# Loading the queries of an attention kernel in one transfer over 128 partitions, and moving them to their places with VectorE copies

## The chip, the cores and the metric

The kernel runs on one core of a Trainium2 chip. The metric is the device time of one execution in microseconds (us); a time is the median of several runs. The kernel before took 639.06 us (3 runs, 638.83 to 639.22). A ratio of two kernels is the mean time of one kernel's fast runs over that of the other's fast runs of the same rounds, so it is not quite the ratio of the medians that are quoted.

## The reference

The reference is plain softmax attention with few queries and many keys: 128 heads (8 x 16), 16 queries each, 2048 keys and values each, head size 256, all in bf16.

```python
B, H, Sq, Skv, Dh = 8, 16, 16, 2048, 256
def reference(q, k, v):
    scale = q.shape[-1] ** -0.5
    scores = jnp.einsum('bhqd,bhkd->bhqk', q, k) * scale
    attn = _softmax(scores, axis=-1)
    return jnp.einsum('bhqk,bhkd->bhqd', attn, v)
```

K and V are 134 MB each, the queries 1.05 MB, the output 1.05 MB. Every byte of K and V is used once (the page counts 269.48 MB read from HBM), and the work is mostly moving bytes: DMA is 72% of the chain that ended last.

## The kernel before

The kernel handles 8 heads at a time (a group g of 16), in two halves e = 0, 1 ("units", u = 2g + e) of 4 MB of K and 4 MB of V each. All K and V loads are issued by SyncE, in one order, each waiting only until its place in SBUF is free. A K load may start when VectorE has transposed the K that was in its place (`kt`); a V load when TensorE has used up the V before it.

```python
qx = q.rearrange("b h s d -> (b h s) d").rearrange("(u a s) d -> a u (s d)", a=4, s=SQ)
...
QR = VB[:, 1, 0:SQ, :].rearrange("p s d -> p (s d)")     # the raw queries, in a V buffer not yet used

def emit_qload(eng, a):                                   # head 4u+a goes to partition 32a+u
    return eng.dma_start(QR[32 * a:32 * a + 2 * G, :], qx[a])

def emit_qt(eng):                                         # VectorE: transposes each 32x32 block
    return eng.transpose(QT[:].bitcast(F32), QR.bitcast(F32))
...
j_q = [J(("sp", "sp", "act", "act")[a], "ldq", lambda eng, a=a: emit_qload(eng, a), [j_qz], dma=(sem_q, 64)) for a in range(4)]
...
# K, groups 0 and 1: two halves of 2 MB per unit; later groups: one load of 4 MB
[("kt", g - 1, e, 2 * h + 1)] if g else []                # what a K load waits for
# order on VectorE at the start: qt, then kt(0, e, c) for both units, then the first row maximum
```

The queries thus come in four loads: load `a` takes every fourth head (32 KB apart in HBM, 8 KB each) and writes the 32 partitions from 32a on. Two of them are issued by SyncE ahead of all K loads, two by ScalarE. After the transpose, ScalarE scales the queries into the weights of TensorE (`qwb`), 8 instructions per group.

## Time and profile before

| what | value | where |
|---|---|---|
| time | 639.06 us | runs |
| span of the profiled run | 637.7 us | page, head |
| TensorE, VectorE, ScalarE busy | 76%, 67%, 15% | page, part 1 |
| DMA | 90% or more in all slices but the first and the last | page, part 2 |
| rate, whole span | 424 GB/s | page, part 2 |

From the page of the kernel before, the head and two rows of part 2 (the span in 40 slices of 16 us: busy tenths of the DMA engines, and what they moved):

```profile
span 637.7 us, 5071 instructions
DMA  8999999999999999999999999999999999999996
GB/s 311 429 443 428 426 430 440 430 438 434 432 428 432 432 428 432 430 430 430 431 443 438 432 430 429 430 432 432 428 432 430 440 432 430 432 436 430 417 423 274
```

The stream runs at about 430 GB/s everywhere except in the first and last slice. The DMA part of the same kernel (operation, count, KB each, median us from issue to landing) shows how deep the queue is:

```profile
KN<-in_k_dram SPq DMA_DIRECT2D x28, 4096.0 KB, 30.0
VB<-in_q_dram SPq DMA_DIRECT2D x2, 256.0 KB, 5.0
VB<-in_q_dram ACTq DMA_DIRECT2D x2, 256.0 KB, 6.9
```

A K load of 4 MB lands 30.0 us after its issue, though 4 MB take 9.7 us at 430 GB/s: some 20 us of earlier loads stand ahead of it. By this estimate a compute engine that runs a few us late in the middle does not starve the DMA engines. What can count is a hole in the stream, and the first slice (311 GB/s) has one.

The windows of 1 us from 3 us on, kernel before. Columns: window, its length, then busy us and instruction counts of TensorE, weight loads, VectorE, ScalarE and GpSimd, the TensorE clock, the busy share of the DMA engines, and GB/s:

```profile
3.00:4.00 1.00, 0.00 (x0) 0.00 (x0) 0.00 (x0) 0.00 (x0) 1.00 (x1) 1.00 1.11 295
4.00:5.00 1.00, 0.00 (x0) 0.00 (x0) 0.00 (x0) 0.00 (x0) 0.91 (x1) 1.00 1.07 254
5.00:6.00 1.00, 0.00 (x0) 0.00 (x0) 0.00 (x0) 0.00 (x0) 0.00 (x0) 1.00 1.02 238
6.00:7.00 1.00, 0.00 (x0) 0.00 (x0) 0.00 (x0) 0.00 (x0) 0.00 (x0) 1.00 1.09 270
7.00:8.00 1.00, 0.00 (x0) 0.00 (x0) 0.00 (x0) 0.00 (x0) 0.00 (x0) 1.00 0.93 328
```

The last two columns are the point: the DMA engines count as fully busy, yet move 238 to 328 GB/s, 55 to 76% of the 430 GB/s of later. So here a busy share near 1 does not tell that transfers go at full rate; only the bytes do.

The start in order of time, kernel before (start us, us, engine, line, operation, count, and in brackets the idle time before it and what ended it):

```profile
0.73 0.86 SPq L110 DMA_DIRECT2D VB<-in_q_dram  x2
0.73 0.90 ACTq L110 DMA_DIRECT2D VB<-in_q_dram  x2
1.64 31.96 SPq L212 DMA_DIRECT2D KN<-in_k_dram  x8
9.72 2.31 DVE L113 STREAM_TRANSPOSE QT<-VB 128x2048 f32<-128x2048 f32 x1 [7.65 <-DMA VB<-in_q_dram]
12.07 3.45 ACT L122 ACTIVATE QW<-QT 32x128 bf16<-32x128 bf16 x8 [9.11 <-DVE QT L113]
14.01 4.50 DVE L128 STREAM_TRANSPOSE KB<-KN 128x2048 f32<-128x2048 f32 x2 [1.98 <-DMA KN<-in_k_dram]
18.58 0.61 PE L145 MATMUL S_ps<-KB,QW 128*128 128x512 bf16 x1 [18.58 <-DVE KB L128]
```

The queries arrive only at 9.7 us and the first K half at 14.0. The end of the chain that ended last (start us, us, what):

```profile
593.87 30.26 DMA KN<-in_v_dram
624.27 10.79 PE O_ps L178 x96
```

After the V piece that lands at 624.1 us TensorE works without a break for 10.8 us, and 2.6 us later the program is over. So the start of this last piece of work follows the stream, and the time follows it.

### The profile page before, as it was taken

What the parts mean: (1) busy time and instruction counts of PE and PEld (TensorE: products, weight loads), DVE (VectorE), ACT (ScalarE), POOL (GpSimd) and SP (SyncE); (2) the same over time, 40 slices, a digit from 0 to 9 for tenths busy, and PEclk for the clock granted to TensorE, in tenths of its full rate; (3) what the DMA queues carried; (4) which work ended last, traced back from release to release, by engine and by line L of the source; (5) the groups of instructions that cost most, each with busy time, mean ns of one, the idle gap of its engine ahead of it and who ended that gap; (6) DMA issues with size and microseconds to landing.
All of it is one profiled execution on the core that took longest, in us unless ns stands there. A gap on an engine that the chain in (4) does not pass through costs nothing.

```text
span 637.7 us, 5071 instructions
## 1 busy us (share of the span) xinstructions
PE 485.4 (76%) x2176; PEld 165.5 (26%) x1680; DVE 428.3 (67%) x371; ACT 93.8 (15%) x176; POOL 4.2 (1%) x7
## 2 busy tenths in 40 slices
PE   0747858959599595986959779596895949959897
PEld 0101312314122140321303113131231312314286
DVE  3979494775947669386683957749477594766960
ACT  2030301103020030300303002030120302103010
POOL 2000000000000000000000000000000000000000
PEclk9979998969989798997979979699897998979999
DMA  8999999999999999999999999999999999999996
GB/s 311 429 443 428 426 430 440 430 438 434 432 428 432 432 428 432 430 430 430 431 443 438 432 430 429 430 432 432 428 432 430 440 432 430 432 436 430 417 423 274
DMA packets 13766, 270.62 MB, mean 424 GB/s; under 512 B 1600, under 2 KB 3904, under 8 KB 4416
## 3 DMA queue, kind: packets, MB, share of 16 engines
q1 hardware_dynamic: 13248, 269.83, 98.9%
q10 hardware_dynamic: 512, 0.70, 0.4%
q8 instruction: 4, 0.07, 0.0%
q14 instruction: 2, 0.02, 0.0%
HBM read 269.48 MB, written 1.05 MB: 424 GB/s over the span
## 4 chain that ended last, share of the span: by engine, by line
DMA 72%; DVE 18%; issue 5%; PE 4%; ACT 0%; SPq 0%; DVEq 0%; ACTq 0%
DMA KN<-in_k_dram 67%; DVE KB L128 17%; DMA KN<-in_v_dram 5%; PE O_ps L178 2%; PE S_ps L145 1%; PE S_ps L133 1%; DVE negm L150 0%; ACT QW L122 0%; SPq L110 0%; DVE O_fin L326 0%; SPq L230 0%; DVEq L481 0%; ACT P_sb L154 0%; ACTq L122 0%; ACTq L484 0%
## 5 line engine op out<-in xcount | busy, mean ns | idle before, releaser
L128 DVE STREAM_TRANSPOSE KB<-KN 128x2048 f32<-128x2048 f32 x128 | 284.8, 2281 | 57.1 <-DMA KN<-in_k_dram 56.1
L145 PE MATMUL S_ps<-KB,QW 128*128 128x512 bf16 x528 | 214.3, 414 | 138.3 <-DMA VB<-in_v_dram 95.0
L133 PE MATMUL S_ps<-KB,QW 128*128 128x512 bf16 x496 | 204.8, 413 | 0.0
L172 PE MATMUL O_ps<-VB,PT 128*128 128x512 bf16 x896 | 195.6, 379 | 9.9 <-DMA VB<-in_v_dram 9.9
L145 PEld LDWEIGHTS S_ps<-KB,QW 128*128 128x128 bf16 x528 | 54.0, 103 | 342.4 <-issue 278.8
L172 PEld LDWEIGHTS O_ps<-VB,PT 128*128 128x128 bf16 x896 | 86.7, 98 | 121.6 <-issue 19.0
L150 DVE TENSOR_REDUCE negm<-S_ps 128x1 f32<-128x2048 f32 x16 | 36.7, 2292 | 86.9 <-PE S_ps L133 86.9
L154 ACT ACTIVATE P_sb<-S_ps,negm 128x2048 bf16<-128x2048 f32 x16 | 31.5, 1967 | 410.5 <-DVE negm L150 410.5
L158 DVE STREAM_TRANSPOSE PC<-P_sb 128x1024 bf16<-128x1024 bf16 x32 | 37.9, 1222 | 33.8 <-ACT P_sb L154 33.8
L164 DVE COPY PT<-PC 32x1024 bf16<-32x1024 bf16 x128 | 53.5, 418 | 3.4 <-PE O_ps L178 1.7
L122 ACT ACTIVATE QW<-QT 32x128 bf16 (+1 forms) x128 | 54.0, 422 | 10.4 <-DVE QT L113 9.1
L315 ACT ACTIVATE O_tmp<-O_ps,rab 128x256 f32<-128x256 f32 x15 | 7.1, 473 | 96.9 <-issue 96.9
L178 PE MATMUL O_ps<-KN,PT 128*128 128x256 bf16 x128 | 14.4, 273 | 1.1 <-DMA KN<-in_v_dram 1.1
L178 PE MATMUL O_ps<-VB,PT 128*128 128x256 bf16 x128 | 14.1, 273 | 0.4 <-DVE PT L164 0.4
L178 PEld LDWEIGHTS O_ps<-KN,PT 128*128 128x128 bf16 x128 | 12.4, 98 | 3.0 <-issue 1.3
L178 PEld LDWEIGHTS O_ps<-VB,PT 128*128 128x128 bf16 x128 | 12.4, 98 | 2.3 <-DVE PT L164 0.8
L326 DVE TENSOR_SCALAR O_fin<-O_ps,rab 128x256 bf16<-128x256 f32 x2 | 1.0, 484 | 12.8 <-PE O_ps L178 6.6
L320 DVE SCALAR_TENSOR_TENSOR O_fin<-O_ps,rab,O_tmp 128x256 bf16<-128x256 f32 x15 | 6.7, 448 | 1.8 <-issue 1.8
L113 DVE STREAM_TRANSPOSE QT<-VB 128x2048 f32<-128x2048 f32 x1 | 2.3, 2311 | 7.7 <-DMA VB<-in_q_dram 7.7
L297 DVE TENSOR_SCALAR rab<-mask,rinv 128x2 f32<-128x2 f32 x16 | 3.7, 228 | 1.5
L191 POOL MEMSET PT<- 128x4096 f32 x1 | 3.5, 3511 | 0.0
L301 DVE COPY rab<-rab 128x2 f32<-128x2 f32 x15 | 2.5, 167 | 1.2
(11 smaller groups left out, 8.4 us busy)
## 6 DMA issues: line engine op xcount, KB each, us to landing
VB<-in_v_dram SPq DMA_DIRECT2D x28, 4096.0 KB, 24.3
KN<-in_k_dram SPq DMA_DIRECT2D x28, 4096.0 KB, 30.0
KN<-in_k_dram SPq DMA_DIRECT2D x8, 2048.0 KB, 15.0
VB<-in_v_dram SPq DMA_DIRECT2D x4, 2048.0 KB, 17.4
KN<-in_v_dram SPq DMA_DIRECT2D x2, 2048.0 KB, 28.0
KN<-in_v_dram SPq DMA_DIRECT2D x2, 1024.0 KB, 24.6
KN<-in_v_dram SPq DMA_DIRECT2D x3, 512.0 KB, 27.2
out_dram<-O_fin SPq DMA_DIRECT2D x13, 64.0 KB, 29.8
```

Of the source, the lines that this page charges most:

```text
L122: ins = eng.activation(ap_of(dv, dv.offset + 32 * a + e, [[256, 4], [128, 2], [2, 16]]), src.rearrange("p (s b) t -> p b t s", b=4), ACTF. ...
L128: return eng.transpose(KBf[:, c % R_KB].rearrange("p t i -> p (t i)"), KNf[:, e].rearrange("p t i -> p (t i)")[:, n * c:n * c + n])
L133: return eng.add_instruction(mybir.InstMatmult(start_tensor_calc=start, stop_tensor_calc=stop, ldweights=False, tile_size=(128, 128), tile ...
L145: ins = mm(S_ps[:, 2 * h + c, :], QW[:, e, bp, :], rhs, start=(e == 0 and bp == 0), stop=(e == 1 and bp == 7))
L150: return eng.tensor_reduce(out=negm[:], in_=S_ps[:].rearrange("p c n -> p (c n)"), axis=AX.X, op=ALU.max, negate=True)
L154: return eng.activation(P_sb[:], S_ps[:].rearrange("p c n -> p (c n)"), ACTF.Exp, bias=negm[:], scale=1.0, accum_out=lsum[:])
L158: return eng.transpose(PC[:, h].rearrange("p t x -> p (t x)"), P_sb[:, 1024 * h:1024 * h + 1024])
L164: ins = eng.tensor_copy(PT[pr, 32 * h:32 * h + 32, pr], PC[pr, h])
L172: ins = eng.matmul(O_ps[:, 0, :], PT[:, t, :], rhs, start=(t == 0), stop=(t == NT - 1))
L178: ins = eng.matmul(O_ps[:, bank, 0:D], PT[:, t, :], buf[:, t, :], start=(t == 0), stop=(t == NT - 1))
L315: j_ea[g] = J("act", "ea", lambda eng: eng.activation(O_tmp[:], src, ACTF.Copy, scale=rab[:, 0, 0:1]), [("pv", g, 1) if g < last - 1 else ...
L320: j_eb[g] = J("dve", "eb", lambda eng: eng.scalar_tensor_tensor(out=O_fin[:, 0, :], in0=src, scalar=rab[:, 0, 1:2], in1=O_tmp[:], op0=ALU. ...
```

## The change

Intent: let the queries come in one load, a head to a partition, straight and contiguous, over all 128 partitions. The transpose of 32x32 blocks (one instruction, 2.31 us) then leaves them in the wrong 32 partitions, so VectorE copies them, 32 partitions at a time, to the places where the scaling expects them: four copies per four groups of heads, 16 in all, the first four before the K transposes, the rest in places where VectorE was expected to wait.

```diff
-    qx = q.rearrange("b h s d -> (b h s) d").rearrange("(u a s) d -> a u (s d)", a=4, s=SQ)
+    qx = q.rearrange("b h s d -> (b h) (s d)")
...
-        def emit_qload(eng, a):
-            return eng.dma_start(QR[32 * a:32 * a + 2 * G, :], qx[a])
         def emit_qt(eng):
-            return eng.transpose(QT[:].bitcast(F32), QR.bitcast(F32))
+            return eng.transpose(QN[:].bitcast(F32), QR.bitcast(F32))
+        def emit_qc(eng, x):
+            src = QN[32 * x:32 * x + 32, :].bitcast(F32).rearrange("p (y v a) -> p y v a", v=8, a=4)
+            for a in range(4):
+                dst = QT[32 * a:32 * a + 32, :].bitcast(F32).rearrange("p (y u) -> p y u", u=32)
+                ins = eng.tensor_copy(dst[:, :, 8 * x:8 * x + 8], src[:, :, :, a])
+            return ins
...
-        j_q = [J(("sp", "sp", "act", "act")[a], "ldq", lambda eng, a=a: emit_qload(eng, a), [j_qz], dma=(sem_q, 64)) for a in range(4)]
+        j_q = [J("sp", "ldq", lambda eng: eng.dma_start(QR[0:NH, :], qx), [j_qz], dma=(sem_q, 16))]
...
-                             [("qt", 0), j_qwz, ("qk", g - 1, 1, 1) if g else None])
+                             [("qc", g // 4), j_qwz, ("qk", g - 1, 1, 1) if g else None])
...  # on VectorE: qc(0) after qt; qc(1) before the first row maximum; qc(2), qc(3) at the end of group 1
-                            mine = dict(k) if jb.cls in ("ld", "ldq", "st") else {**prev[e], **k}
+                            mine = dict(k)
+                            if jb.cls not in ("ld", "ldq", "st"):
+                                mine.update((key, val) for key, val in prev[e].items() if k.get(key, 0) < val)
```

The last hunk belongs to the part that plans which waits can be left out; it takes a few waits out of the loops of VectorE and ScalarE. Slots and slices of the loops move along.

More of the change, by code (lines that the diff above doesn't have):

```diff
@@ L14 @@
 R_KB = 4
-PE_SLOT, DVE_SLOT, ACT_SLOT = 8, 144, 80
+PE_SLOT, DVE_SLOT, ACT_SLOT = 8, 160, 80
 STEP = 16
@@ L54, in bass_standalone__softmax_full_bidir__sampling_kernel @@
         QT = ec(nc.sbuf_tensor("QT", [128, SQ * D], BF16))
+        QN = ec(nc.sbuf_tensor("QN", [128, SQ * D], BF16))
         QW = ec(nc.sbuf_tensor("QW", [128, 2, 8, 128], BF16))
@@ L193, in bass_standalone__softmax_full_bidir__sampling_kernel @@
         j_mask = J("dve", "mask", emit_mask, [j_ident])
-        j_qz = J("dve", "qz", lambda eng: eng.memset(QR.bitcast(F32), 0.0)) if 2 * G < 32 else None
-        j_q = [J(("sp", "sp", "act", "act")[a], "ldq", lambda eng, a=a: emit_qload(eng, a), [j_qz], dma=(sem_q, 64)) for a in range(4)]
+        j_qz = J("dve", "qz", lambda eng: eng.memset(QR.bitcast(F32), 0.0)) if NH < 128 else None
+        j_q = [J("sp", "ldq", lambda eng: eng.dma_start(QR[0:NH, :], qx), [j_qz], dma=(sem_q, 16))]
         j_k, j_v, j_kt, j_qk, j_pv = {}, {}, {}, {}, {}
         j_qwb, j_qt, j_exp, j_pt, j_px, j_max, j_rab = {}, {}, {}, {}, {}, {}, {}
-        j_ea, j_eb, j_st, j_rold = {}, {}, {}, {}
+        j_ea, j_eb, j_st, j_rold, j_qc = {}, {}, {}, {}, {}
         vparts = {NU - 4: [32, 32], NU - 3: [32, 32], NU - 2: [32, 32], NU - 1: [16, 16, 8, 8, 8, 4, 2, 2]}
@@ L366, in bass_standalone__softmax_full_bidir__sampling_kernel, with qc @@
         j_qt[0] = J("dve", "qt", emit_qt, j_q)
+        def qc(x):
+            if 32 * x < NH:
+                j_qc[x] = J("dve", "qc", lambda eng: emit_qc(eng, x), [("qt", 0)])
+        qc(0)
         for g in range(G):
@@ L379, in bass_standalone__softmax_full_bidir__sampling_kernel @@
                 px(g - 1, 1)
+            if g == 0:
+                qc(1)
             dve_max(g)
@@ L386, in bass_standalone__softmax_full_bidir__sampling_kernel @@
             small(g)
+            if g == 1:
+                qc(2)
+                qc(3)
         dve_tail = len(order["dve"])
@@ L396, in bass_standalone__softmax_full_bidir__sampling_kernel @@
         tables = {"kt": j_kt, "qwb": j_qwb, "qt": j_qt, "qk": j_qk, "exp": j_exp, "pt": j_pt, "px": j_px, "max": j_max,
-                  "rab": j_rab, "rold": j_rold, "ea": j_ea, "eb": j_eb, "st": j_st, "pv": j_pv}
+                  "rab": j_rab, "rold": j_rold, "qc": j_qc, "ea": j_ea, "eb": j_eb, "st": j_st, "pv": j_pv}
         def resolve(d):
@@ L405, in bass_standalone__softmax_full_bidir__sampling_kernel @@
                  "pe": [order["pe"][0:4]] + [order["pe"][6 * x - 2:6 * x + 4] for x in range(1, last)],
-                 "act": [order["act"][3:5]] + [order["act"][3 * x + 2:3 * x + 5] for x in range(1, last)]}
-        n_tail = {"dve": dve_tail, "pe": 6 * last - 2, "act": 3 * last + 2}
+                 "act": [order["act"][1:3]] + [order["act"][3 * x:3 * x + 3] for x in range(1, last)]}
+        n_tail = {"dve": dve_tail, "pe": 6 * last - 2, "act": 3 * last}
         def plan():
```

## The prediction

> **What bounds the kernel now.** DMA. The page's slices show the DMA engines at 90% or more in all but the first and last of 40, at about 430 GB/s. In the middle, landings repeat every 39.03 us for 16.8 MB of K and V. K loads take 30.0 us from issue to landing, though 4 MB need 9.7 us at that rate: some 20 us of work is always queued ahead. VectorE is busy 67%, TensorE 76%. Only a hole in the DMA stream can count.
>
> **Where there is a hole: the start.** In windows of 1 us the DMA engines are about 100% busy from 3 us on, but move 295, 254, 238, 270 and 328 GB/s from 3 to 8 us, and 393 to 442 afterwards. Up to 9 us they moved 2.05 MB; 430 GB/s from the first packet (1.76 us) would be 3.1 MB: about 2.4 us lost. In the packet records the 8 KB query packets first take 0.31 us, then 0.50 to 0.58 us. [...] One engine also fetches 16 KB of instructions at 3.2 us (1.70 us); there queries landed last, at 9.2 us, and one engine stays 1.2 to 1.7 us behind the median to the end, and so sets most landings.
>
> **What the change does.** Removes three query issues (0.4 us each; K's first issue moves from 1.64 to about 1.2 us) [...]. Adds on VectorE 16 copies of 32 x 512 f32, 4 of them before the first ScalarE scaling. Estimate 0.4 to 0.65 us each, from the 32x1024 bf16 copies at 0.42 us: 1.6 to 2.6 us at the head, 8 to 10 us in all. The loops lose some waits; no value there.
>
> Head after (estimates): queries on all engines by 5 to 6 us (9.7 before), transpose 2.3 us, copies to about 10.5 us; first K half (13.9 us before) at about 11 us. So the copies hide behind K's landing; the scaling (3.45 us) ends by 14, before the first two K transposes (4.5 us) at 15.5. First matmul at about 15.8 us instead of 18.6. The second group of copies falls into VectorE's wait for TensorE (33 to 37 us). The last two (some 4 us, near 73 us) delay one K transpose by about 2 us; the queue is deep enough.
>
> **On the critical path:** only the DMA stream's head. The median engine finishes the first K half at 11.7 us; without the conflict about 9.6: 2.0 us. The late engine may gain 0.5 more. The shift is carried unchanged to the end, where the tail (last V pieces, TensorE's 10.8 us) moves with it.
>
> **Predicted:** 636.8 us, 80% range 635.9 to 638.2. Faster by over 2%: 0.01; within 2%: 0.98; slower by over 2%: 0.01.
>
> **What would show it.** Right: about 400 GB/s from 3 to 9 us, first slice about 370 instead of 311; 8 KB packets near 0.31 us; first K transpose at 11 us; period still 39.03 us. Wrong: packets still at 0.5 us [...]; copies over 1 us each, holding the first matmul; a slower period.
>
> **What would make it wrong.** The instruction fetch falling on another engine or being longer; the late engine's lag coming back later, so that the gain shrinks to 1 us; a V load issued late after the 73 us copies, with a starved queue.

The sum behind the forecast: 639.06 us less the 2.0 us of the stream and part of the 0.5 us of the late engine, 2.26 us together, is 636.8 us. "The conflict" is the slow stretch at the start (238 to 328 GB/s from 3 to 8 us); "about 9.6" is an estimate (the queries and the first K half, 3.15 MB, at 430 GB/s from the first packet at 1.76 us would be done at 9.1 us). That it was the engine with the instruction packet on which the queries landed last is inferred from the times; the records do not name the engine. By the landing records of the kernel before, the last engine was 1.6 to 2.0 us behind the median in all K and V loads.

## The result, and the profile after

The changed kernel took 636.91 us (6 runs, 636.81 to 636.96) against 639.08 us (6 runs, 638.83 to 639.24) on the same chip; the ratio is 0.9966, with an interval of 0.9953 to 0.9979. That is 2.17 us, as predicted (2.26 us).

The same rows of the page, after:

```profile
span 635.5 us, 5055 instructions
DMA  8999999999999999999999999999999999999997
GB/s 364 430 432 437 442 431 429 433 429 431 431 431 431 431 429 433 429 433 429 433 430 431 433 429 433 429 429 433 437 425 439 435 429 439 427 440 429 414 424 280
```

Only the first slice differs clearly: 364 instead of 311 GB/s. 53 GB/s over 15.9 us are 0.84 MB, and 0.84 MB at 430 GB/s are 2.0 us. The same windows, after:

```profile
3.00:4.00 1.00, 0.00 (x0) 0.00 (x0) 0.00 (x0) 0.00 (x0) 1.00 (x1) 1.00 1.13 467
4.00:5.00 1.00, 0.00 (x0) 0.00 (x0) 0.00 (x0) 0.00 (x0) 0.91 (x1) 1.00 1.02 418
5.00:6.00 1.00, 0.00 (x0) 0.00 (x0) 0.00 (x0) 0.00 (x0) 0.00 (x0) 1.00 1.10 467
6.00:7.00 1.00, 0.00 (x0) 0.00 (x0) 0.00 (x0) 0.00 (x0) 0.00 (x0) 1.00 1.01 434
7.00:8.00 1.00, 0.00 (x0) 0.00 (x0) 0.90 (x1) 0.00 (x0) 0.00 (x0) 1.00 0.92 393
```

The share of the DMA engines is what it was; the bytes are not. The start in order of time, after:

```profile
0.74 0.38 SPq L201 DMA_DIRECT2D VB<-in_q_dram  x1
1.18 15.68 SPq L217 DMA_DIRECT2D KN<-in_k_dram  x5
7.10 2.31 DVE L110 STREAM_TRANSPOSE QN<-VB 128x2048 f32<-128x2048 f32 x1 [5.03 <-DMA VB<-in_q_dram]
9.45 2.44 DVE L117 COPY QT<-QN 32x512 f32<-32x512 f32 x4
11.99 4.50 DVE L133 STREAM_TRANSPOSE KB<-KN 128x2048 f32<-128x2048 f32 x2
16.55 0.10 PEld L150 LDWEIGHTS S_ps<-KB,QW 128*128 128x128 bf16 x1 [16.55 <-DVE KB L133]
```

The queries come 2.6 us earlier and the transpose and the four copies fit in before K: the copies end at 11.89 us. The last DMA engine finished the first K half at 11.47 us (13.49 before), the semaphore of this half was complete at 11.90 us (13.92 before), and VectorE began K 0.09 us after that in both kernels (11.99 and 14.01). So the copies are hidden, but with nothing to spare: they and the landing end at the same time. The whole cost of the copies, from the groups of the page (count, busy us, mean ns):

```profile
L117 DVE COPY QT<-QN 32x512 f32<-32x512 f32 x16 | 9.7, 606 | 0.3
```

And the end of the chain:

```profile
591.84 30.00 DMA KN<-in_v_dram
621.97 10.82 PE O_ps L183 x96
```

TensorE's last stretch begins 2.30 us earlier and is as long as before. The middle only hands the gain on. This table is worked out from the packet records of the traces: the time at which the DMA engines had moved so many MB in all (every packet of the trace is counted, also the few that carry instructions).

| MB moved | before, us | after, us | difference |
|---|---|---|---|
| 1 | 6.20 | 5.09 | 1.11 |
| 3.1 (queries and the first K half) | 11.92 | 10.06 | 1.86 |
| 10 | 28.19 | 26.19 | 2.00 |
| 100 | 237.11 | 235.18 | 1.93 |
| 250 | 584.53 | 582.61 | 1.92 |
| 269.5 | 629.72 | 627.71 | 2.01 |

The gain is made before 12 us and then carried for 620 us without loss. The remaining 0.2 to 0.3 us come from the one DMA engine that is behind the others. By the semaphore records (16 landings per load, read here as one for each of the 16 DMA engines) the median engine finished the last V piece at 622.21 us before and at 620.19 us after (2.02 us earlier), the last engine at 624.14 and 621.84 us (2.30 us earlier), and the last stretch of TensorE waits for the last engine. How far this engine is behind differs from kernel to kernel (1.3 to 3.4 us at this piece in the runs quoted below); why was not found.

The packet records also show where the time went. A packet of queries is one row of 8 KB, a head. Before, the median took 0.51 us, and 98 of 128 took more than 0.45 us; after, the median took 0.31 us (26 GB/s on one engine; 16 engines at this rate are 423 GB/s), and 13 took more than 0.45 us, most of them the first ones. The K packets behind them were slow too before: of the K packets that began before 9 us, 42 of 60 took over 0.7 us, after 1 of 109.

### The profile page after: what moved, and what is told of

It reads as the page before. It is cut to its first block, busy times and chain, and to the rows that moved or that the text cites. A ratio compares the mean times of both kernels' runs of the same rounds, so it can differ in the third digit from the quotient of the medians.

```text
span 635.5 us, 5055 instructions
## 1 busy us (share of the span) xinstructions
PE 485.9 (76%) x2176; PEld 165.5 (26%) x1680; DVE 437.5 (69%) x387; ACT 93.7 (15%) x176; POOL 4.2 (1%) x7
## 2 busy tenths in 40 slices
DMA packets 13718, 270.62 MB, mean 426 GB/s; under 512 B 1552, under 2 KB 3856, under 8 KB 4368
## 4 chain that ended last, share of the span: by engine, by line
DMA 74%; DVE 18%; issue 5%; PE 3%; SPq 0%; DVEq 0%; ACT 0%; ACTq 0%
DMA KN<-in_k_dram 65%; DVE KB L133 16%; DMA KN<-in_v_dram 5%; DMA VB<-in_v_dram 4%; PE O_ps L183 2%; DVE QT L117 1%; PE S_ps L150 1%; PE S_ps L138 1%; DVE PC L163 0%; DVE negm L155 0%; SPq L217 0%; DVE O_fin L331 0%; SPq L201 0%; SPq L235 0%; DVEq L499 0%
## 5 line engine op out<-in xcount | busy, mean ns | idle before, releaser
L117 DVE COPY QT<-QN 32x512 f32<-32x512 f32 x16 | 9.7, 606 | 0.3
L110 DVE STREAM_TRANSPOSE QN<-VB 128x2048 f32<-128x2048 f32 x1 | 2.3, 2311 | 5.0 <-DMA VB<-in_q_dram 5.0
```

Source lines behind the costliest of these rows:

```text
L117: ins = eng.tensor_copy(dst[:, :, 8 * x:8 * x + 8], src[:, :, :, a])
```

## The experiments

Twelve more kernels ran, on two chips, each beside the kernel before on the same chip. The theory: the partitions that a load writes decide. Packets of a load into 32 neighbouring partitions are slow (median 0.51 us before, 0.31 us after the change), and so are the K packets among them (42 of 60 over 0.7 us before, 1 of 109 after). The reason that the author had for this is shown by no trace or run and is cut, with the theory's name, from the expectations below; what stands after such a cut is what the theory expected. The profile shows how long packets take, not why. Rivals: the source in HBM (rows 32 KB apart), the number of loads and their issue time, the second queue, and the waits taken out of the loops.

| kernel | time, us (runs) | before in the same rounds, us | queries' packets, median us | 3.1 MB moved at, us |
|---|---|---|---|---|
| changed kernel | 636.91 (6) | 639.08 | 0.31 | 10.06 |
| a_four_two_queues | 639.13 (5) | 639.16 | 0.56 | 11.94 |
| a_four_strided | 637.93 (5) | 639.16 | 0.31 | 10.58 |
| b_new_waits | 639.20 (5) | 639.16 | 0.54 | 12.07 |
| a_two_halves | 639.56 (5) | 639.30 | 0.62 | 12.49 |
| a_two_combed | 638.22 (5) | 639.30 | 0.31 | 10.33 |
| a_four_one_queue | 639.77 (4) | 639.30 | 0.61 | 11.96 |
| a_all_at_head | 640.18 (5) | 639.16 | 0.31 | 9.99 |
| a_eight_at_head | 637.25 (4) | 639.30 | 0.31 | 9.98 |
| a_q_on_act | 639.30 (4) | 639.23 | 0.31 | 9.84 |
| b_permuted_source | 661.23 (4) | 639.23 | 0.76 | 19.82 |
| b_x4_narrow | 651.12 (4) | 639.23 | 0.50 | 14.21 |
| a_x4_wide | 644.45 (4) | 639.23 | 0.31 | 9.95 |

All gave correct results. Names that begin with a are variants of the changed kernel, those with b of the kernel before.

### Four narrow loads put back: a_four_two_queues

```diff
-        j_q = [J("sp", "ldq", lambda eng: eng.dma_start(QR[0:NH, :], qx), [j_qz], dma=(sem_q, 16))]
+        j_q = [J(("sp", "sp", "act", "act")[a], "ldq", lambda eng, a=a: eng.dma_start(QR[32 * a:32 * a + 32, :], qx[32 * a:32 * a + 32, :]),
+                 [j_qz], dma=(sem_q, 64)) for a in range(4)]
```

> The changed kernel, but the queries come in four loads of 32 partitions (two from SyncE, two from ScalarE, as before the change), each from a contiguous 256 KB of HBM. [...] 8 KB packets at 0.50 to 0.58 us again, first K half on the median engine near 11.8 us instead of 10.0, and 638.7 to 639.2 us: the gain is gone. Rival that the pattern in HBM (every fourth head, 32 KB apart) made the old loads slow: 636.9 us, since the source is contiguous here. Rival that the shorter wait lists or the moved loops gave the gain: 636.9 us.

639.13 us against 639.16: the whole gain is gone (ratio 0.9999, 0.9985 to 1.0013), though the source is contiguous, the copies are there and the loops have the new waits. Packets took 0.56 us. The source pattern, the waits and the loops are not what gave the gain.

### Only the waits: b_new_waits

The kernel before with the last hunk of the change alone.

> The kernel before with only the changed rule for which waits are left out (fewer waits in the loops). [...] 639.0 us, nothing changes. Rival that the waits gave the gain: 636.9 us.

639.20 against 639.16 us (ratio 1.0, 0.9987 to 1.0014): nothing, and the interval, 0.9 us to either side, leaves no room for a gain of 2 us.

### Four loads to every fourth partition: a_four_strided

```diff
-  QR[32 * a:32 * a + 32, :], qx[32 * a:32 * a + 32, :]      (as in a_four_two_queues)
+  QR[a:128:4, :], qx[a:128:4, :]
```

> The changed kernel, four loads of 32 partitions from two queues, but each load goes to every fourth partition[...]; its source is every fourth head, 32 KB apart, exactly that of the kernel before. [...] packets mostly near 0.31 us and 636.9 to 637.6 us[...]. Rival that the number of loads, the second queue, or the source pattern makes the old start slow: 638.7 to 639.2 us.

Packets are back at 0.31 us, with four loads of 32 partitions from two queues and with the very source pattern of the kernel before. 3.1 MB were moved at 10.58 us. The time, 637.93 us (637.26 to 638.33), is 1.2 us better than before, but 1.0 us short of the changed kernel, a miss of the tighter part of the expectation. Half a us of that stands in the stream: the two issues took 1.22 us on SyncE, so K's first issue came at 2.00 instead of 1.18 us, and 27 of 93 early K packets took over 0.7 us. The profiled run, at 637.26 us the fastest of the five, is only 0.3 us above the profiled run of the changed kernel (636.96 us), no more than the stream explains. Why the other four took up to 1.1 us longer is open: they have no profile.

### Twins of two loads: a_two_halves and a_two_combed

These two differ only in which heads each load takes, and so in the partitions that it writes and the rows that it reads (neighbouring ones, or every second):

```diff
 j_q = [J("sp", "ldq", lambda eng, a=a: ..., [j_qz], dma=(sem_q, 32)) for a in range(2)]
-        eng.dma_start(QR[64 * a:64 * a + 64, :], qx[64 * a:64 * a + 64, :])     # a_two_halves
+        eng.dma_start(QR[a:128:2, :], qx[a:128:2, :])                           # a_two_combed
```

> The changed kernel with the queries in two loads from SyncE: partitions 0 to 63, then 64 to 127. [...] packets at 0.5 us or more, 3.1 MB moved about 1.9 us later than in the changed kernel (12.0 instead of 10.1 us), 638.5 to 639.2 us. Rival that many loads (issue time, per-load cost) were the matter: one issue more than in the changed kernel, 0.4 us: 637.3 us.

> The same two loads from SyncE with the same sizes, but the even partitions first, then the odd ones[...]. [...] packets at 0.31 us, 636.9 to 637.5 us, well below its twin of two halves. Rival (number of loads, or rows of 64): the same time as the twin.

This is the cleanest pair: same queue, sizes, number of issues and issue times (queries from 0.74 us, K from 2.00 and 2.01 us). That the rows read in HBM are not the matter is shown by the other kernels: contiguous rows were slow in a_four_two_queues, and rows 32 KB apart were fast in a_four_strided. Windows of 1 us, a_two_halves (columns as above; the last two are DMA share and GB/s):

```profile
3.00:4.00 1.00, 0.00 (x0) 0.00 (x0) 0.00 (x0) 0.00 (x0) 1.00 (x1) 1.00 1.06 262
4.00:5.00 1.00, 0.00 (x0) 0.00 (x0) 0.00 (x0) 0.00 (x0) 0.92 (x1) 1.00 1.17 254
5.00:6.00 1.00, 0.00 (x0) 0.00 (x0) 0.00 (x0) 0.00 (x0) 0.00 (x0) 1.00 1.19 262
```

And a_two_combed:

```profile
3.00:4.00 1.00, 0.00 (x0) 0.00 (x0) 0.00 (x0) 0.00 (x0) 1.00 (x1) 1.00 0.97 393
4.00:5.00 1.00, 0.00 (x0) 0.00 (x0) 0.00 (x0) 0.00 (x0) 0.91 (x1) 1.00 1.02 426
5.00:6.00 1.00, 0.00 (x0) 0.00 (x0) 0.00 (x0) 0.00 (x0) 0.00 (x0) 1.00 1.21 483
```

Packets took 0.62 against 0.31 us, two to one; 3.1 MB were moved at 12.49 against 10.33 us; times 639.56 (639.42 to 639.83) against 638.22 us (637.74 to 638.45). Which partitions a load writes decides; why was not shown. It need not be one load over all partitions: these two loads of every second partition, and four of every fourth in a_four_strided, span the 128 partitions without filling them, and had packets of 0.31 us, against 0.62 and 0.56 us for neighbouring partitions. As with a_four_strided, the combed loads stay 1.3 us behind the single load in time though only 0.27 us of it stands in the stream at 3.1 MB, so the expected 636.9 to 637.5 us was missed. In the profiled run (637.74 us, again the fastest of its five) the rest is the engine that is behind: the last V piece was complete on the median engine at 620.45 us, 0.26 us later than in the changed kernel, and on the last engine at 622.66 us, 0.82 us later. That is the 0.8 us by which this run is longer than the profiled run of the changed kernel.

### Four narrow loads from one queue: a_four_one_queue

> The changed kernel with four loads of 32 partitions, all from SyncE, contiguous source. [...] the second queue is not needed for the loss: packets at 0.5 us or more, 638.7 to 639.5 us (K is also issued 1.2 us later, which the queries' own 2.4 us or more hide). Rival that the two queues taking turns at one engine made the loss: 637 us.

639.77 us, packets 0.61 us. The second queue is not needed for the loss. (The kernel before, with one queue on partitions 0 to 63 and the other on 64 to 127, fares little better, 0.51 us.)

### The cost magnified: b_x4_narrow and a_x4_wide

The queries are loaded four times, into four places of the same idle buffer, before K.

```diff
-  for a in range(4)]                                   # b: 4 loads of 32 partitions
+  for j in range(4) for a in range(4)]                 # b_x4_narrow: 16 of them
-  [one load]                                           # a: 1 load of 128 partitions
+  [the same load for j in range(4)]                    # a_x4_wide: 4 of them
```

> The kernel before, loading the queries four times (into four different places, 16 loads of 32 partitions, two queues): the disputed cost, magnified. Three more MB. [...] each MB takes about 4.2 to 4.9 us of the stream [...]: 639.1 + 3 x 4.2 to 4.9 = 651.7 to 653.8 us. Rival that the old start lost its 2 us once, to start-up or issue: each MB costs 2.43 us (1.049 MB at 431 GB/s): 646.4 us.

> The changed kernel, loading the queries four times, each as one load of 128 partitions. Both theories: each further MB costs 2.43 us: 636.9 + 7.3 = 644.2 us. More would mean that the wide load has a fixed cost too.

Each further load of the queries (1.049 MB) cost (651.12 - 639.23) / 3 = 3.96 us narrow, and (644.45 - 636.91) / 3 = 2.51 us wide (636.91 is from other rounds), where 1.049 MB at 431 GB/s are 2.43 us. So the loss comes again with every load and is not paid once. It is 1.45 us per further load: less than the 1.8 to 2.5 us of the expectation (4.2 to 4.9 us narrow, estimate, against 2.43 us), and less than the 2.0 us that the stream gained by the change. What makes the first load dearer was not found.

### How much room do the copies have? a_all_at_head and a_eight_at_head

```diff
-        qc(0)
+        for x in range(4):       # a_all_at_head;   a_eight_at_head: qc(0), qc(1)
+            qc(x)
```

> The changed kernel with all 16 copies (0.60 us each) ahead of the first K transpose: VectorE starts K about 7.3 us later (near 19.3 instead of 12.0 us). If only the DMA stream counts and its queue holds: 636.9 us, within 0.3. The queue holds 8 MB, until about 24.6 us on the median engine; the fifth K load is then issued at about 24 us, so it is close: a hole of at most 1 to 2 us, 636.9 to 638.5. Rival that the start of compute sets the time: 636.9 + 7.3 = 644 us.

> The changed kernel with 8 of the 16 copies ahead of the first K transpose: K transposes begin near 14.4 us instead of 12.0, as late as in the kernel before. The first K half then frees its place at about 19.0 us, and the queued loads last until 24.6 us: 636.9 us, within 0.3. With the 16 copies at the head (19.3 us: 640.2) and the queries from ScalarE (17.6 us: 639.3) this gives the threshold: a start of K up to some 17 us should cost nothing. Rival that every us of later start costs a share of a us: 637.7 to 638.2 us.

With 8 copies at the head VectorE begins K at 14.28 us instead of 11.99, and the stream is as before: 10 MB moved at 26.15 us (26.19 in the changed kernel), 250 MB at 582.50 (582.61). The median was 637.25 us; two runs were at 636.82 and 636.95, two at 637.55 and 638.69, for which there is no profile. So a free delay of 2.3 us is shown for the profiled run (636.95 us); the median misses the expected 0.3 us narrowly, and a cost in part of the executions is not excluded. The "threshold" of some 17 us in the expectation is an estimate: shown are a start of K at 14.28 us without loss, and losses at 17.60 us (a_q_on_act) and 19.32 us. With 16 copies, VectorE in order of time:

```profile
9.41 9.88 DVE L117 COPY QT<-QN 32x512 f32<-32x512 f32 x16
19.32 8.89 DVE L133 STREAM_TRANSPOSE KB<-KN 128x2048 f32<-128x2048 f32 x4
```

K begins at 19.32 us, and the four K loads already in the queue run out at 24.5 us (median engine) before the fifth, issued at about 24 us, brings anything. 10 MB were moved 1.10 us later, 20 MB 2.13 us, 269.5 MB 2.54 us, and the time is 640.18 us, 3.3 us above the changed kernel. The expectation of a hole of 1 to 2 us was too small: not only the fifth, but also the following K loads were late, since each waits for the transposes in its turn (SyncE waited 34.4 us for them with the K loads of the first two groups, 26.8 us in the changed kernel).

### Queries from ScalarE, K first: a_q_on_act

```diff
-        j_q = [J("sp", "ldq", ...
+        j_q = [J("act", "ldq", ...
```

> The changed kernel with the one query load issued from ScalarE, so that SyncE issues K at once (0.74 instead of 1.18 us) and the two streams share the engines from the start. The stream's bytes are the same, so 636.9 us within 0.3; up to 0.5 us less if the slow first packets (1.3 us each) overlap with K's. Queries land later (8 to 10 instead of 6.6 us), first matmul near 17.5 to 18 us instead of 16.55. Rival that the first matmul's time matters: 1 us slower.

This missed. The start of the stream is slightly better, 3.1 MB at 9.84 us, but the two queues had about equal shares (from 3 to 10 us 118 packets of queries and 122 of K began), so the queries, though 1.049 MB at 431 GB/s would be 2.4 us, were not complete before 11.7 us. VectorE took its work in the order of the program: transpose at 12.79, copies at 15.13, K at 17.60 us. What SyncE waited for (us in total, times, longest), changed kernel:

```profile
SPq L217 <- DVE KB L133: 26.8, 4, 13.2
```

And a_q_on_act:

```profile
SPq L217 <- DVE KB L133: 33.5, 4, 19.5
```

The K loads of group 1 were issued 6 us later, the stream fell back by 0.67 us at 20 MB and 1.04 us at 40 MB, and TensorE's last stretch began 3.0 us later than in the changed kernel in the profiled run (639.94 us, the slowest of four; median 639.30). The last V piece was complete on the median engine at 621.45 us, 1.26 us later than in the changed kernel, and on the last engine at 624.87 us, 3.03 us later: the rest of the 3.0 us is the engine that is behind, by 3.4 instead of 1.7 us; why was not found. So the early arrival of the queries is a condition of the gain: in the profiled runs the queue covered a start of K at 14.3 us, not one at 17.6 us.

### No copies, by permuting the source: b_permuted_source

One load of 128 partitions, whose source lists the heads in the final order (a, u), so that no copies are needed.

```diff
-            return eng.dma_start(QR[32 * a:32 * a + 2 * G, :], qx[a])
+            return eng.dma_start(QR, qx)          # qx is (a u (s d)): a = 4, u = 32
```

> The kernel before with one load of 128 partitions whose source is permuted, so that every head lands in its final place and no copies are needed. [...] 640 to 644 us. If all 16 engines carry it: 636.9 us, as the changed kernel without its copies.

661.23 us, 22 us worse, far more than expected. The pages show that this load was carried differently: packets under 512 B, read here as the completions, are 1600 for the 100 loads and stores before (16 each), 1552 for 97 after, but 1540 here, which is 96 x 16 + 4. So this load had 4 completions instead of 16, read here as 4 engines instead of 16. Windows of 4 us, b_permuted_source:

```profile
8.00:12.00 4.00, 0.00 (x0) 0.00 (x0) 0.00 (x0) 0.00 (x0) 0.00 (x0) 1.00 1.03 207
12.00:16.00 4.00, 0.00 (x0) 0.00 (x0) 0.00 (x0) 0.00 (x0) 0.00 (x0) 1.00 0.96 152
20.00:24.00 4.00, 0.00 (x0) 0.00 (x0) 0.00 (x0) 0.00 (x0) 0.00 (x0) 1.00 0.89 139
```

The 128 packets of queries, 32 for each of four engines, took 0.76 us in the median (0.31 in the changed kernel); 32 of them are some 24 us. The last one ended at 28.6 us, and from 4 to 28 us the whole stream moved 139 to 231 GB/s. The K packets beside them were slow as well (median 1.23 us before 9 us, 0.61 in the changed kernel). Why both were so slow is open; the number of engines alone would give 10 us (an estimate: 32 packets of 0.31 us).

## Why the prediction was right, point by point

- "Only a hole in the DMA stream can count": right. 9.7 us of new VectorE work and changed loops moved nothing (the period of landings in the middle is still 39.02 us, 39.02 before), and the 2 us won before 12 us arrived at the end.
- The narrow loads as the cause: shown by the twins (0.62 against 0.31 us per packet) and by the four narrow loads put back (no gain left). So it is a matter of the partitions written; the reason for it was not shown.
- The signs named beforehand came: first slice 364 GB/s (about 370 predicted), 442 GB/s from 3 to 9 us (about 400), packets of 0.31 us.
- Size of the stream's gain, predicted 2.0 us: 1.86 us at 3.1 MB, 2.0 us at the end. On the median engine the first K half was done at 10.01 us, not 9.6: eight of the first nine packets took 0.87 to 1.33 us, and from 2 to 3 us the new kernel moved only 131 GB/s (221 before). This was left out.
- The late engine, "may gain 0.5 more": direction right, size smaller. It gained 2.02 us at the first K half (13.49 to 11.47) where the median engine gained 1.79, and TensorE's last stretch began 2.30 us earlier where the stream gained 2.01. It still lags: 1.46 us behind the median at the first K half, 1.65 us at the last V piece (1.93 before). The prediction gave no reason why it should lag less, so that this part fitted, and with it that the total came within 0.1 us, is partly luck. The packet of instructions that the prediction tells of (16 KB) took 1.70 us at 3.2 us before and 0.96 us at 3.6 us after, and by the first K half one engine was 1.7 and 1.5 us behind the median; it did not catch up. The records do not name the engine, but the times fit: in the kernel after, the packet of queries from which the late ones follow began at 4.57 us, as the packet of instructions ended. It is not the whole of the lag: in a_four_strided, where that packet came at 1.95 us, the last engine was 0.5 us behind at the first K half but 1.3 us at the last V piece.
- Copies of 0.4 to 0.65 us: 0.61 us. Queries by 5 to 6 us: 6.6 us on the last engine, transposed from 7.1. Copies done "by 10.5": 11.9. First K transpose "at 11": 12.0. First matmul "15.8": 16.55 (18.58 before). Each step was about 1 us late, and none counted, for the reason given: K is a few us of queue away from mattering (a_eight_at_head, in its profiled run).
- The copies near 73 us: they ran from 70.95 to 75.95 us, as expected, and had no effect on the stream.

## What to carry to other kernels

In these runs a load into 32 or 64 neighbouring partitions took 0.50 to 0.62 us per packet of 8 KB instead of 0.31 us, and the packets of other loads beside it were slower too (42 of 60 K packets over 0.7 us, 1 of 109 beside the wide load), while the DMA engines showed as fully busy; read the GB/s, not the share. In a kernel bound by its stream, find where the stream has a hole, and check with the bytes moved by a given time whether a change there is carried to the end. What is moved to an idle engine in exchange is free only as long as the loads already queued outlast it: here a delay of 2.3 us cost nothing in the stream of the profiled run, one of 7.3 us cost 3.3 us.
